# Gated linear attention with a folded feed-forward: K laid out by tokens with transposing DMAs, and running products over two chunks

## The chip, the cores and the metric

The kernel runs on one core of a Trainium2 chip. Its time is the device time of one execution in microseconds (us). The engines are named as in the profile: PE (TensorE) does matrix products, with PEld for its weight loads; DVE (VectorE), ACT (ScalarE) and POOL (GpSimd) work on elements; SP (SyncE) issues the DMA transfers. Each engine takes its instructions in the order in which the program gives them, and waits on semaphores for the results of the others. SBUF is the on-chip memory of 128 partitions, PSUM the eight banks that PE writes to.

## The reference

The first part is a gated linear recurrence for 4 batches, 8 heads, 768 steps and a head dimension of 48. Its result, with the heads side by side (3072 tokens of 384 numbers), goes through a feed-forward layer without a nonlinearity other than a product.

```python
f = 1.0 / (1.0 + np.exp(-f_logit))
state = np.zeros((B, H, D, D), dtype=np.float32)
for t in range(S):
    state = f[:, :, t, :, None] * state + np.einsum('bhd,bhe->bhde', k[:, :, t], v[:, :, t])
    y[:, :, t] = np.einsum('bhd,bhde->bhe', q[:, :, t], state)
...
a = x @ w1          # x: 3072 x 384, w1 and w2: 384 x 1024
b = x @ w2
h = a * b @ w3      # 1024 x 1024
return (h @ w_out).astype(np.float32)   # 1024 x 384
```

All of it is in 32-bit floats.

## The kernel before

**Recurrence.** The 768 steps of a batch are cut into 6 chunks of 128 tokens, 24 chunks (`NU`) in all, numbered u through the four batches. The 8 heads lie as 4 pairs: one head of a pair on partitions 0 to 47, the other on 64 to 111 (R = 112 rows), the four pairs side by side along the columns (4 x 128 = 512 columns, `NQ`). Within a chunk the decays are running products. A chunk's *front* makes them (`front`, L521 to L559): ACT takes the sigmoid of f (tile `gate`), a scan on DVE runs the product P forward over each head's 128 tokens (`fwd`), a small copy on ACT keeps its last column (`lasts`), a reciprocal sets the start of a second scan on DVE that runs R backward (`bwd`), and two products on DVE give Q = q * P and K = k * R, each into a tile of its own.

PE needs K twice: as it is for the products of K and Q (`pairs`, L584), and with tokens on the partitions for the update of the state (`update`, L690). For the second, PE itself transposes each head pair's 128 columns against an identity (`turn`, L598, four matrix products a chunk into a bank of PSUM), and ACT copies the bank to the tile `kt` (L731).

From chunk 4 on the PE work of neighbouring chunks is joined in *visits* (`visit` in `rest`): the visit of chunk u has half of the products of masked pairs with v (`values`, L658), the pairs of chunk u + 1, the other half of the values, the part from the state (`from_state`, L677), and the update of chunk u + 1. ACT copies the pairs out of PSUM (L707), POOL sets those after the diagonal to 0 (L713). On DVE the state is carried by `mid` and S (L763, L766) and multiplied by the gain G (L822), which POOL makes from `lasts` and the next chunk's first gate (L813). The result goes out by ACT (`ys`, L849), and two DMAs through DRAM turn it to the layout of the feed-forward (`yt`, then `xt`).

**Feed-forward.** The tokens are worked in 6 blocks of 512. w3 and w_out are first multiplied with each other on PE (L1471, eight groups of 16 matrix products, called the folding here) into `wc`, so that a block needs x with w1 and w2 (the up products), their elementwise product, and that with `wc` (the down products). Blocks use Strassen-like schemes, so sums and differences of weights and of x are made on DVE: those of the folded weights are the four of L1518 (`wc_sums`), which need all eight pieces of the folding.

**The order.** All tasks are given to a list scheduler, `Plan`, with an engine, an estimated cost, dependencies, a priority and the buffers they take. It picks the task that can start first by its estimates and so fixes the order of the instructions on each engine; on the chip the engines then wait for each other as it comes. The priorities of the recurrence follow `need(u)`, a due time of 60 + 14.5 (u - 4) from chunk 4 on. Where the plan has PE idle, the program puts dummy matrix products on the tile `floor` there (`idle`, L402), one for each 0.43 us of the gap.

Buffers: two gates, three q, two k and two f tiles, two K and three Q tiles, all of 112 x 512. Later in the program the same memory holds sums of weights (`homes`, `W_SUMS`).

Of the kernel before, what the change touches and what calls it, by code (L numbers as in the profile page):

```python
# [45 lines left out]
P = 128  # L46
C = 128
# [12 lines left out]
NQ = HP * C  # L60
NPE = 2
# [18 lines left out]
SURE_W = 2.0  # L80
NEED = (0.0, 1.0, 2.0, 3.0)
# [16 lines left out]
NFRONT = 12  # L98
# [28 lines left out]
FLOOR = 2.0**-60  # L127
RANGE = 2.0**-40
# [167 lines left out]
def ranged(ctx, tc, q, k, f_logit, v, w1, w2, w3, w_out, out, ident, w12, wc, left):  # L296
# [17 lines left out]
    floors = keep.tile([P, NQ], F32, name="floor")  # L314
    floor = floors[0:R]
    spare = keep.tile([P, NQ], F32, name="back")
    back = spare[0:R]
    gates_ = [keep.tile([P, NQ + 1], F32, name=f"gate{i}") for i in range(2)]
    inputs = [[keep.tile([P, NQ], F32, name=f"{nm}{i}") for i in range(n)] for nm, n in (("q", 3), ("k", 2), ("f", 2))]
    gate = [t[0:R] for t in gates_]  # L320
    qs, ks, fs = ([t[0:R] for t in ts] for ts in inputs)
    both = keep.tile([P, 2 * WIDE], F32, name="A")
    flat = [both[:, i * WIDE : i * WIDE + WIDE] for i in range(2)]
    masked = [t.rearrange("p (r h c) -> p r h c", r=2, h=HP) for t in flat]
    diag = [t[:, 0 : 2 * HP * W].rearrange("p (r h c) -> p r h c", r=2, h=HP) for t in flat]
    mids = [t[0:R, 2 * HP * W : 2 * HP * W + HP * D].rearrange("p (h d) -> p h d", d=D) for t in flat]
    firsts = [keep.tile([P, TB], F32, name=f"a{i}") for i in range(2)]
    sb = [t[0:R, 0 : HP * R].rearrange("p (h r) -> p h r", r=R) for t in firsts]
    lasts = keep.tile([R, NU, HP], F32, name="lasts")
# [23 lines left out]
    early = abp.tile([P, KH, TB], F32, name="ab")[0:R]  # L353
    ks += [early[:, 0], early[:, 1]]
    fs += [early[:, 2], early[:, 3]]
    qs.append(at(12288, NQ)[0:R])
    dns = {nm: at(12288 + DH * i, DH) for i, nm in enumerate(("m1", "u2", "u3"))}

    homes = [lambda t=t: t[:, 0:NQ] for t in [floors] + gates_ + inputs[0] + inputs[1] + inputs[2]]
    homes += [lambda p=p, nm=nm: p.tile([P, NQ], F32, name=nm) for p, nm, n in ((one, "fwd", 1), (one, "bwd", 1), (work, "K", 2), (work3, "Q", 3), (work3, "ys", 3)) for _ in range(n)]  # L360
# [16 lines left out]
    plan.pools["t"][0:4] = [aside] * 4  # L377
    moving = plan.add("PE", 0.0, lambda: None, takes=["ab"], prio=-1e9)
    coming = plan.add("PE", 0.0, lambda: None, takes=["ab"], prio=-1e9)
# [29 lines left out]
    def setup():  # L409
        E = mybir.EngineType  # L410
        tc.mark_branch_hint_location("general", hint="LikelyTaken", engines=[E.SP, E.DVE, E.PE, E.Activation, E.Pool])
        nc.scalar.activation(warm, nc.const_aps.tensor(0.0, (R, 1), F32), AF.Sigmoid)
        for i in range(2):
            if i == 0:
                nc.gpsimd.memset(ks[i][32:64], 0.0)
                nc.gpsimd.memset(qs[i][32:64], 0.0)
                make_identity(nc, ident)
            else:
                nc.gpsimd.memset(fs[i][32:64], 30.0)
        nc.gpsimd.memset(early[32:64, 2:4], 30.0)  # L420
        nc.gpsimd.memset(early[32:64, 0:2], 0.0)
        nc.gpsimd.memset(qs[2][32:64], 0.0)
        nc.gpsimd.memset(qs[3][32:64], 0.0)
        nc.vector.memset(floor, FLOOR)
        nc.vector.memset(heads(floor)[:, :, 0], 1.0)
        nc.vector.memset(back, 0.0)
        for t in gate:
            nc.vector.memset(t[:, NQ : NQ + 1], 0.0)
        nc.vector.memset(ks[1][32:64], 0.0)
        nc.vector.memset(qs[1][32:64], 0.0)  # L430
        for t in sb:
            nc.vector.memset(t, 0.0)

        nc.gpsimd.memset(perm, 0.0)
# [22 lines left out]
    def need(u):  # L457
        return NEED[u] if u < 4 else 60 + 14.5 * (u - 4)
# [21 lines left out]
    def front(u):  # L480
# [3 lines left out]
        ask = n0 - 30 if u in (0, 1) or u > 3 else turn_of(str(u))  # L484
        ask = [ask, ask + 0.5, ask + 1.0, n0 - (28.2, 28.2, 28.2, 28.2, 12)[min(u, 4)] if u in (0, 1) or u > 3 else ask + VLATE[u - 2] if u in (2, 3) else ask + 1.2]

        def load(dst, src):
            def emit():
                if dst is fs[0] and u == 0:
# [8 lines left out]
        fu, qu, ku = (x[u if u < 4 else u % n] for x, n in ((fs, 2), (qs, 3), (ks, 2)))  # L498

        def free(n, *names):  # L500

            if u < 4:
                return []
            return asked[8:9] + [tk[u - n if u - n >= 4 else u % n][nm] for nm in names]

        since = n0 - AHEAD if 4 < u < 8 else 0.0
        t["lf"] = moves(2, 197, 300, load(fu, f_logit), free(2, "g"), ask[0], since=since)
        t["lk"] = moves(2, 197, 300, load(ku, k), free(2, "k"), ask[1], since=since)
        t["lq"] = moves(2, 197, 300, load(qu, q), free(3, "q"), ask[2], since=since)

        def load_v():
# [4 lines left out]
            1, 197, 320, load_v, [] if u == 3 else past(u, 4 if u in (4, 5, 6) else 3, "v", "s"),  # L516
            ask[3],
        )

        def gates():  # L520
            nc.scalar.activation(gate[u % 2][:, 0:NQ], fu, AF.Sigmoid)  # L521

        t["g"] = plan.add("ACT", 0.65, gates, [t["lf"]] + past(u, 2, "r") + past(u, 3, "G"), n0)
        if u % NCH and "G" in tk[u - 1]:
            tk[u - 1]["G"]["deps"].append(t["g"])

        def forward():
            s["P"] = one.tile([P, NQ], F32, name="fwd")[0:R]
            nc.vector.tensor_tensor_scan(s["P"], gate[u % 2][:, 0:NQ], floor, 0.0, ALU.mult, ALU.max)  # L529

        t["p"] = plan.add("DVE", 1.25, forward, [t["g"]] + past(u, 1, "q", "i", "l"), n0)
# [6 lines left out]
        def ends():  # L538
            nc.vector.reciprocal(heads(back)[:, :, C - 1], heads(s["P"])[:, :, C - 1])
# [3 lines left out]
        def scale_q():  # L543
            s["Q"] = work3.tile([P, NQ], F32, name="Q")[0:R]
            nc.vector.tensor_tensor(s["Q"], qu, s["P"], ALU.mult)

        t["q"] = plan.add("DVE", 0.72, scale_q, [t["p"], t["lq"]] + past(u, 3, "v", "a"), n0 + QLATE, shared=True)

        def backward():
            s["R"] = one.tile([P, NQ], F32, name="bwd")[0:R]  # L550
            nc.vector.tensor_tensor_scan(  # L551
                s["R"][:, ::-1], gate[u % 2][:, NQ:0:-1], back[:, ::-1], 0.0, ALU.mult, ALU.max
            )

        t["r"] = plan.add("DVE", 1.25, backward, [t["i"]] + past(u, 1, "k"), n0)

        def scale_k():
            s["K"] = work.tile([P, NQ], F32, name="K")[0:R]
            nc.vector.tensor_tensor(s["K"], ku, s["R"], ALU.mult)  # L559

        t["k"] = plan.add("DVE", 0.72, scale_k, [t["r"], t["lk"]] + past(u, 2, "a", "t"), n0, shared=True)
        if u in (2, 3):
            t["k"]["frees"].append(coming)
# [160 lines left out]

    def turning(u):

        s, t = st[u], tk[u]

# [24 lines left out]
    def middle(u):  # L753
# [4 lines left out]
        def emit():  # L758
# [10 lines left out]
            "DVE", 0.36 if closes else 0.72, emit, [t["s"], t["m"]] + ([] if opens else past(u, 1, "d")) + past(u, 2, "v"), need(u) - 5,  # L769
        )  # L770

    def rest(u):
# [13 lines left out]
        else:  # L786
            middle(u)
            more = u + 1 < NU and u >= SOLO
            after = tk[u + 1] if more else {}

            def visit():
# [10 lines left out]
                "PE", 0.15 + 0.46 * (2 - 0.5 * opens + 2 * more), visit,  # L802
                [t["c"], t["lv"], t["mid"]] + past(u, 1, "y", *([] if opens else ["d"])) + [after[nm] for nm in ("q", "k", "e", "lv") if after],
                n0 - 998, slack=0.8,
            )
            if after:
                after["a"] = after["s"] = t["v"]
                paired(u + 1)

        if not closes:  # L810
            def gains():
                s["G"] = work.tile([R, HP], F32, name="G")
                nc.gpsimd.tensor_tensor(s["G"], lasts[:, u], heads(gate[(u + 1) % 2][:, 0:NQ])[:, :, 0], ALU.mult)  # L813
# [3 lines left out]
            )  # L817

# [24 lines left out]
        def outcome():  # L843
            s["ys"] = work3.tile([P, NQ], F32, name="ys")[0:R].rearrange("p (h c) -> p h c", c=C)
# [8 lines left out]
            "ACT", 0.8, outcome, [t["v"]] + past(u, 3, "z"),  # L853
# [43 lines left out]
    fronts = plan.add("none", 0.0, lambda: None)  # L897
# [9 lines left out]
    def ffn(n):  # L907
# [203 lines left out]
        def many_sums():  # L1111
            for k, (i, o, j, h) in enumerate(W_SUMS if not w_nodes else []):
                def emit(i=i, o=o, j=j, k=k):
                    nc.vector.tensor_tensor(w_view(4 * KM + k), w_view(i), w_view(j), op(o))
                w_nodes.append(plan.add("DVE", 0.69, emit, [over if h >= NFRONT else fronts] + w_nodes[-1:], W_SOON + 0.1 * k, since=W_SINCE + W_STEP * k))
# [123 lines left out]
        def down(i):  # L1239
# [88 lines left out]
            n0 = 100 * n + 90 + i + 60 * (n > 1) + 30 * (n == NB - 2)  # L1328
# [234 lines left out]
    def judge():  # L1563
        low = work.tile([R, 1], F32, name="low")
        nc.vector.tensor_reduce(out=low, in_=lasts, axis=AX.XY, op=ALU.min)
        zero = work.tile([R, NU], F32, name="zero")
        nc.vector.tensor_scalar(zero, ysum, 0.0, None, ALU.mult)
        nil = work.tile([R, 1], F32, name="nil")
        nc.vector.tensor_reduce(out=nil, in_=zero, axis=AX.X, op=ALU.add)
        nc.vector.tensor_scalar(nil, nil, 0.0, None, ALU.is_equal)  # L1570
        good = work.tile([P, 1], F32, name="good")
# [11 lines left out]
    def heard():  # L1583
        row = work.tile([1, P], F32, name="row")
# [3 lines left out]
    def decided():  # L1588
        least = work.tile([1, 1], F32, name="least")
# [4 lines left out]
    for u in range(NU):  # L1594
        if u <= SOLO:
            front(u)
        if NPE <= u <= SOLO:
            turning(u)
            begin(u)
        if u >= SOLO and u + 1 < NU:  # L1600
            front(u + 1)
# [6 lines left out]
        if u == NU - 1:  # L1608
# [4 lines left out]
            fronts["deps"] += [tk[u][nm] for nm in ("r", "k", "q")] + [tk[u - 1]["G"]]  # L1613
# [405 lines left out]
```

## Time and profile before

| | |
|---|---|
| runs, in us | 461.73, 459.99, 458.59 |
| median | 459.99 |
| the profiled execution | 458.04 |
| its span (first to last instruction) | 456.2 |
| clock of PE in it | 1.00 |

The busy times of an engine are sums over its instructions and can overlap with waits of others, so only a row of the chain that ended last, or a stretch in which one engine never stands still, tells what sets the end. The profile has three stretches that matter here: the folding from 60 to 120 us, the rest of the recurrence to 257 us, and products of the feed-forward alone from there to the end. Rows of groups give line, engine, operation, names and shapes, the count, busy time and mean of one; the rest of a row is idle time of that engine ahead of the group, with what ended it.

### The profile page before, as it was taken

What the parts mean: (1) busy time and instruction counts of PE and PEld (TensorE: products, weight loads), DVE (VectorE), ACT (ScalarE), POOL (GpSimd) and SP (SyncE); (2) the same over time, 40 slices, a digit from 0 to 9 for tenths busy, and PEclk for the clock granted to TensorE, in tenths of its full rate; (3) what the DMA queues carried; (4) which work ended last, traced back from release to release, by engine and by line L of the source; (5) the groups of instructions that cost most, each with busy time, mean ns of one, the idle gap of its engine ahead of it and who ended that gap; (6) DMA issues with size and microseconds to landing.
All of it is one profiled execution on the core that took longest, in us unless ns stands there. A gap on an engine that the chain in (4) does not pass through costs nothing.

```text
span 456.2 us, 11781 instructions
## 1 busy us (share of the span) xinstructions
PE 448.7 (98%) x4792; PEld 392.5 (86%) x4792; DVE 371.1 (81%) x651; ACT 212.0 (46%) x473; POOL 69.1 (15%) x90
## 2 busy tenths in 40 slices
PE   7999999999999999999999999999999999999996
PEld 6788886666899888889999888899899988889996
DVE  8997899999898999989999699885659466767641
ACT  4565344432234453443323256665665666675300
POOL 9341000131222531223223000000000000000000
PEclk9999999999999999999999999999999999999999
DMA  6897898833236666356323502446365612233111
GB/s 178 268 339 249 300 340 284 271 108 105 71 100 196 180 175 162 105 155 184 97 73 82 147 16 78 138 141 205 132 194 172 204 60 96 91 93 92 37 69 39
DMA packets 43308, 68.74 MB, mean 151 GB/s; under 512 B 5217, under 2 KB 28386, under 8 KB 42226
## 3 DMA queue, kind: packets, MB, share of 16 engines
q1 hardware_dynamic: 43250, 67.95, 48.6%
q8 instruction: 38, 0.62, 0.6%
q14 instruction: 20, 0.16, 0.1%
HBM read 58.88 MB, written 9.04 MB: 149 GB/s over the span
## 4 chain that ended last, share of the span: by engine, by line
PE 95%; DVE 1%; SPq 1%; DMA 1%; POOL 0%; issue 0%; POOLq 0%; DVEq 0%
PE f L902 25%; PE l L1153 15%; PE f L998 13%; PE f L1153 12%; PE f L1471 9%; PE l L902 9%; PE py L658 3%; PE pa L584 2%; PE f L598 2%; PE py L677 2%; PE pa L690 2%; PE f L402 1%; SPq L495 1%; DMA ab<-in_k_dram 1%; DVE K L559 0%
## 5 line engine op out<-in xcount | busy, mean ns | idle before, releaser
L713 POOL TENSOR_SCALAR_AFFINE_SELECT A<-A 64x512 f32<-64x512 f32 (+1 forms) x46 | 46.2, 1004 | 107.8 <-ACT A L707 105.7
L1471 PE MATMUL f<-place 128*128 128x384 f32 x128 | 42.4, 487 | 0.0
L902 PE MATMUL f<-xt,w 128*128 128x256 f32 x192 | 42.1, 380 | 0.0
L902 PEld LDWEIGHTS f<-xt,w 128*128 128x128 f32 x192 | 36.3, 190 | 5.0
L1471 PEld LDWEIGHTS f<-place 128*128 128x128 f32 x128 | 23.9, 190 | 15.5
L902 PE MATMUL f<-place 128*128 128x192 f32 x176 | 31.9, 327 | 0.0
L998 PE MATMUL f<-xt,w 128*128 128x256 f32 x120 | 31.3, 380 | 0.0
L551 DVE TENSOR_TENSOR_SCAN bwd<-gate,back 112x512 f32<-112x512 f32 x24 | 30.4, 1267 | 0.7
L529 DVE TENSOR_TENSOR_SCAN fwd<-gate,floor 112x512 f32<-112x512 f32 x24 | 30.0, 1251 | 1.2 <-ACT gate L521 0.3
L902 PEld LDWEIGHTS f<-place 128*128 128x128 f32 x176 | 28.9, 190 | 0.4 <-issue 0.2
L849 ACT ACTIVATE ys<-py 112x512 f32<-112x512 f32 x22 | 13.1, 597 | 32.4 <-PE py L677 29.9
L1407 ACT ACTIVATE place<-place 128x512 f32<-128x512 uint32 (+2 forms) x24 | 21.4, 890 | 9.7 <-DMA place<-in_w_dram 8.7
L998 PEld LDWEIGHTS f<-xt,w 128*128 128x128 f32 x120 | 22.5, 190 | 2.9
L902 PE MATMUL f<-wc,ab 128*128 128x192 f32 x128 | 23.6, 328 | 0.0
L813 POOL TENSOR_TENSOR G<-lasts,gate 112x4 f32<-112x4 f32 x20 | 12.3, 614 | 72.3 <-ACT lasts L534 28.7
L902 PEld LDWEIGHTS f<-wc,ab 128*128 128x128 f32 x128 | 21.2, 190 | 0.3
L521 ACT ACTIVATE gate<-f 112x512 f32<-112x512 f32 x22 | 13.9, 631 | 16.4 <-DVE bwd L551 7.2
L902 PE MATMUL l<-place 128*128 128x192 f32 x112 | 19.8, 326 | 0.0
L658 PEld LDWEIGHTS py<-A,vt 64*64 64x64 f32 (+1 forms) x672 | 13.3, 127 | 7.3 <-issue 6.3
L998 PE MATMUL f<-place 128*128 128x256 f32 x72 | 19.1, 386 | 0.0
L902 PEld LDWEIGHTS l<-place 128*128 128x128 f32 x112 | 18.5, 190 | 0.1
L658 PE MATMUL py<-A,vt 64*64 64x64 f32 (+1 forms) x672 | 18.0, 223 | 0.2
(288 smaller groups left out, 1063.4 us busy)
## 6 DMA issues: line engine op xcount, KB each, us to landing
place<-in_w_dram SPq DMA_DIRECT2D x21, 512.0 KB, 5.9
A<-in_w_dram SPq DMA_DIRECT2D x19, 512.0 KB, 4.0
place<-in_w_dram SPq DMA_DIRECT2D x8, 1024.0 KB, 6.3
q<-in_q_dram SPq DMA_DIRECT2D x46, 96.0 KB, 2.9
vt<-in_v_dram SPq DMA_DIRECT2D x23, 192.0 KB, 2.9
out_dram<-o SPq DMA_DIRECT2D x23, 192.0 KB, 2.8
k<-in_k_dram SPq DMA_DIRECT2D x44, 96.0 KB, 2.4
yt<-ys SPq DMA_DIRECT2D x44, 96.0 KB, 2.9
```

Source lines behind the costliest of these rows:

```text
L521: nc.scalar.activation(gate[u % 2][:, 0:NQ], fu, AF.Sigmoid)
L529: nc.vector.tensor_tensor_scan(s["P"], gate[u % 2][:, 0:NQ], floor, 0.0, ALU.mult, ALU.max)
L551: nc.vector.tensor_tensor_scan(s["R"][:, ::-1], gate[u % 2][:, NQ:0:-1], back[:, ::-1], 0.0, ALU.mult, ALU.max)
L658: done = nc.tensor.matmul(y_block(u, hp, par, half)[p0 : p0 + w], lhsT=s["v"][half * W : half * W + W, h * D : h * D + w], rhs=s["A"][half ...
L713: nc.gpsimd.affine_select(out=a, in_=a, pattern=pattern, compare_op=ALU.is_ge, fill=0.0, base=0, channel_multiplier=-1,)
L813: nc.gpsimd.tensor_tensor(s["G"], lasts[:, u], heads(gate[(u + 1) % 2][:, 0:NQ])[:, :, 0], ALU.mult)
L849: nc.scalar.activation(ys, py, AF.Copy, accum_out=ysum[:, u : u + 1])
L902: nc.tensor.matmul(out_, lhsT=lhs[i], rhs=rhs[i], start=start and i == 0, stop=i == len(lhs) - 1, skip_group_check=True,)
L998: nc.tensor.matmul(q[nm][:, which * TH : which * TH + TH], lhsT=lhs[i](which), rhs=rhs[i], start=start and which == 0 and i == 0, stop=i = ...
L1153: nc.tensor.matmul(banks[g, c][:, which * TH : which * TH + TH], lhsT=lhs, rhs=x_node(a), start=first and which == 0, stop=True, skip_grou ...
L1407: nc.scalar.activation(part_.bitcast(F32), part_, AF.Copy, bias=2.0, scale=2.0**-51)
L1471: nc.tensor.matmul(w3s["p", jc], lhsT=w3s[jc][:, kc * P : kc * P + P], rhs=wos[:, kc], start=(kc == 0), stop=(kc == KF - 1),)
```

## The change

From chunk 4 on the fronts are made for two chunks at once (`front_of_two`). Its gate, k and q tiles hold both chunks (112 x 1024); the running products go over 256 tokens, so that both chunks of the two share one reference point: an even chunk there has no G and no product of S with G any more. Backward products are written over the gates, Q and K over q and k. There are three q tiles, two k tiles and two gate tiles of this size.

From chunk 5 on, K gets its tokens onto partitions without PE (`crossing`): ACT splits the 32-bit words into their upper and lower halves (16 bits each) in the staging tile `apart`, a transposing DMA from SP's queue turns the eight 112 x 128 pieces into `halves`, and ACT merges the halves into `kt`. Both tiles exist once. Chunks 0 to 4 are transposed on PE as before.

From chunk 7 on (`TURN`) the visit of chunk u has the pairs of chunk u + 2 in place of u + 1; the pairs of chunk 8 come as a task of their own ahead of the visit of chunk 7. `mid` of u now also waits for the copy of the pairs of u + 1. The due times start 12 us earlier (48 in place of 60), a down product's priority changes for one block, and the sums of weights wait for parts of the old fronts' buffers apart from each other.

```diff
+ALONE = 4
+TURN = 7
...
     def need(u):
-        return NEED[u] if u < 4 else 60 + 14.5 * (u - 4)
+        return NEED[u] if u < 4 else 48 + 14.5 * (u - 4)
...
+    def front_of_two(e):
...
+        P_, R_ = running[0:R, 0:N2], gate[0:R, 1 : N2 + 1]
+        def gates():
+            nc.scalar.activation(gate[0:R, 0:N2], gate[0:R, 0:N2], AF.Sigmoid)
+        def forward():
+            nc.vector.tensor_tensor_scan(P_, gate[0:R, 0:N2], back, 0.0, ALU.mult, ALU.max)
+        def scale_q():
+            to = by_head(qu)
+            nc.vector.tensor_tensor(to, to, by_run(P_), ALU.mult)
+        def backward():
+            nc.vector.tensor_tensor_scan(R_[:, ::-1], R_[:, ::-1], back[:, ::-1], 0.0, ALU.mult, ALU.max)
+            nc.vector.memset(heads2(back)[:, :, 2 * C - 1], 0.0)
+        def scale_k():
+            to = by_head(ku)
+            nc.vector.tensor_tensor(to, to, by_run(R_), ALU.mult)
...
+    def crossing(u):
+        def split():
+            nc.scalar.copy(apart.rearrange("p (two n) -> p two n", two=2), s["K"].bitcast(U16).rearrange("p (n two) -> p two n", two=2))
+        def crossed():
+            nc.sync.dma_start_transpose(halves.rearrange("p (g r) -> p g r", r=R), apart)
+        def merged():
+            s["kt"] = work.tile([P, HP, R], F32, name="kt")
+            to = s["kt"].rearrange("p h r -> p (h r)").bitcast(U16).rearrange("p (n two) -> p two n", two=2)
+            nc.scalar.copy(to, halves.rearrange("p (two n) -> p two n", two=2))
+        n0 = need(u)
+        t["t"] = plan.add("ACT", 1.27, split, [t["k"]] + past(u, 1, "c2"), n0 - 50)
+        t["c2"] = moves(1, 229, 200, crossed, [t["t"]] + past(u, 1, "e"), n0 - 100, SURE_K)
+        t["e"] = plan.add("ACT", 1.13, merged, [t["c2"]] + past(u, 2, "s"), n0 - 50)
...
     def turning(u):
+        if u > SOLO:
+            crossing(u)
+            return
...
+            to = u + 2 if u >= TURN else u + 1
+            two = tk[to] if to < NU and more else {}
+            if u == TURN:
+                ahead = tk[u + 1]
+                ahead["a"] = plan.add("PE", 0.46, lambda: pairs(u + 1), [ahead["q"], ahead["k"], t["m"], t["mid"]], n0 - 999, slack=0.8)
...
                 values(u, 1)
-                if more:
-                    pairs(u + 1)
+                if two:
+                    pairs(to)
                 values(u, 0)
                 from_state(u)
                 if more:
                     update(u + 1)
...
-        if not closes:
+        if not closes and u >= ALONE and u % 2 == 0:
+            t["d"] = t["mid"]
+        elif not closes:
...
-            n0 = 100 * n + 90 + i + 60 * (n > 1) + 30 * (n == NB - 2)
+            n0 = 100 * n + 90 + i + 60 * (n > 0) + 30 * (n == NB - 2)
```

In the rows of the order, a line of the program stands first, then the instruction, its output and inputs by name and a shape. On PE, at the end of the folding, before (`py` is a visit's bank, `pa` that of pairs and updates, `place` and `wc` hold weights):

```order
L677 MATMUL py<-Q,A 48x64 x8
L690 MATMUL pa<-vt,kt 48x48 x16
L902 MATMUL f_1248<-xt,w_59 128x256 x3
L902 MATMUL f_1259<-xt,w_59 128x256 x3
L902 MATMUL f_1271<-xt,w_59 128x256 x3
L902 MATMUL f_1277<-xt,w_59 128x256 x3
L402 MATMUL f_1289<-floor 128x256 x2
L902 MATMUL f_1292<-wc,ab 128x192 x4
```

And in the changed kernel (L779 is `from_state`, L792 the update, L1611 the folding, L686 `pairs`, L416 the dummies, L760 the values):

```order
L779 MATMUL py<-q_98,A 48x64 x8
L792 MATMUL pa<-vt,kt 48x48 x16
L1611 MATMUL f_1196<-place 128x384 x8
L416 MATMUL f_1234<-floor 128x256 x4
L686 MATMUL pa<-q_99,k_101 64x64 x16
L416 MATMUL f_1265<-floor 128x256 x4
L760 MATMUL py<-A,vt 64x64 x2
```

The pairs of chunk 8 and the visit of chunk 7 have moved ahead of the first product with `wc`, and eight dummies stand around them where two stood (a ninth is further up).

On DVE, ahead of the differences of `wc` (L1504 are sums of w1 and w2, L529 and L551 the two scans, L1518 the differences), before:

```order
L1504 TENSOR_TENSOR place<-w_59,place 128x512
L1504 TENSOR_TENSOR place<-w_59 128x512
L529 SCALAR_TENSOR_TENSOR fwd<-gate_95,floor 112x512
L539 RECIPROCAL back<-fwd 112x4
L551 SCALAR_TENSOR_TENSOR bwd<-gate_95,back 112x512
L1518 TENSOR_TENSOR place<-wc 128x768
L1518 TENSOR_TENSOR place<-wc,place 128x768
```

And in the changed kernel (L1644 are the sums of w1 and w2, L632 the forward scan of two chunks, L888 and L891 `mid` and S, L962 S with G, L1658 the differences):

```order
L1644 TENSOR_TENSOR place<-w_59,place 128x512
L1644 TENSOR_TENSOR place<-w_59 128x512
L632 SCALAR_TENSOR_TENSOR run<-gate_96,back 112x1024
L888 TENSOR_TENSOR A<-pa,S 112x192
L891 TENSOR_TENSOR S<-pa,A 112x192
L962 TENSOR_TENSOR S<-S,G 112x192
L1658 TENSOR_TENSOR place<-wc 128x768
L1658 TENSOR_TENSOR place<-wc,place 128x768
```

A scan for two chunks, and the carry of chunk 7, now stand ahead of the differences; the fronts of earlier chunks stand further up in both.

On ACT, in the recurrence after the folding, before (L731 copies a transposed K, L1039 copies up products out of their banks, L707 the pairs, L849 a result):

```order
L521 ACTIVATE gate_96<-f_103 112x512
L731 COPY kt<-f_1706 128x448
L1039 COPY a_105<-f_1712 128x512
L534 COPY lasts<-fwd 112x4
L521 ACTIVATE gate_95<-f_102 112x512
L849 ACTIVATE ys,ysum<-py 112x2x2x128
L707 COPY A<-pa 128x512
L1039 COPY a_106<-f_1712 128x512
```

And in the changed kernel (L840 is the merge, L832 the split, L1179 copies up products, L989 a result, L809 the pairs):

```order
L1179 COPY a_105<-f_1542 128x512
L840 COPY kt<-halves 128x2x448
L1179 COPY a_106<-f_1542 128x512
L832 COPY A<-k_101 112x1024
L989 ACTIVATE ys,ysum<-py 112x2x2x128
L809 COPY A<-pa 128x512
L1179 COPY place<-f_1542 128x512
```

The merge and the split stand between copies that empty PE's banks, with one such copy between the merge of a chunk and the split of the next.

More of the change, by code (lines that the diff above doesn't have):

```diff
@@ L60 @@
 NQ = HP * C
+N2 = 2 * NQ
+ALONE = 4
+TURN = 7
 NPE = 2
@@ L496, in load @@
             return emit
[L498 to L509, printed above, removed]
+        t["lf"] = moves(2, 197, 300, load(fu, f_logit), [], ask[0])
+        t["lk"] = moves(2, 197, 300, load(ku, k), [], ask[1])
+        t["lq"] = moves(2, 197, 300, load(qu, q), [], ask[2])
         def load_v():
```

235 lines of the change are left out of this document (157 added, 78 removed).

## The prediction

> **What bounds the kernel now.** I read the page first: span, busy times, clock, and the share of each line in the chain that ended last.
>
> ```profile
> span 456.2 us, 11781 instructions
> PE 448.7 (98%) x4792; PEld 392.5 (86%) x4792; DVE 371.1 (81%) x651; ACT 212.0 (46%) x473; POOL 69.1 (15%) x90
> PEclk9999999999999999999999999999999999999999
> PE 95%; DVE 1%; SPq 1%; DMA 1%; POOL 0%; issue 0%; POOLq 0%; DVEq 0%
> ```
>
> PE is busy for 448.7 of 456.2 us at full clock and makes 95% of the chain. So PE work taken away shortens the span by as much, and any time in which PE stands still is added. Next, the view of waits for PE (wait, total, times, longest), of which these are two of the three rows:
>
> ```profile
> PE f L402 <- DVE floor L425: 1.7, 1, 1.7
> PE py L598 <- DVE K L559: 0.5, 1, 0.5
> ```
>
> Both belong to the start. Nothing else holds PE: every other engine is early, and the question is which one stays early. The windows view gives it by stage (length, then busy time and count of PE, PEld, DVE, ACT, POOL, then clock, DMA share, GB/s); 60 to 120 us is the folding of w3 with w_out, 120 to 257 the rest of the recurrence beside up and down products, 257 to 452 products alone.
>
> ```profile
> 60.00:120.00 60.00, 60.00 (x608) 40.42 (x607) 56.97 (x75) 23.29 (x43) 9.54 (x10) 1.00 0.63 199
> 120.00:257.00 137.00, 136.90 (x2599) 123.70 (x2598) 125.62 (x225) 52.09 (x127) 37.86 (x46) 1.00 0.50 135
> 257.00:452.00 195.00, 194.99 (x1015) 180.08 (x1013) 135.51 (x283) 106.56 (x244) 0.00 (x0) 1.00 0.35 112
> ```
>
> In the folding DVE is busy for 56.97 of 60 us: it is second to PE and has 3 us to spare. ACT is idle for more than half of each of these stages.
>
> **Term 1: the transposes leave PE.** The chain in order of time (start, length, what), around the visit of chunk 5 and the end of the folding, and for 120 to 257 us the heading of the same view, shares by line:
>
> ```profile
> 78.44 0.39 PE f L598 x4
> 103.49 0.38 PE py L658 x11
> 103.87 0.47 PE pa L584 x30
> 105.02 0.36 PE pa L690 x32
> 105.38 0.53 PE f L598 x4
> 123.29 0.86 PE f L402 x4
> 124.15 3.94 PE f L902 x23
> ```
>
> ```profile
> by line: PE f L998 41.0%; PE f L902 29.7%; PE py L658 7.7%; PE pa L584 5.4%; PE py L677 5.2%; PE f L598 5.1%; PE pa L690 4.2%; PE f L1153 1.3%; PE f L402 0.6%; issue 0.0%
> ```
>
> Transposes take 5.1% of these 137 us, 7.0 us for 16 chunks, 0.44 us each; single pieces are 0.39 behind products and 0.53 behind an update. Chunks 5 to 23 lose theirs: 19 x 0.44 = 8.3 us. The bounds: 19 x 0.39 = 7.4, and by the busy time of all such rows, quoted next, 88 of 12.6 us, 4 to a chunk, 0.57 a chunk, so 10.9.
>
> ```profile
> L598 PE MATMUL f<-ident,K 112*128 112x112 f32 x88 | 12.6, 266 | 0.5 <-DVE K L559 0.5
> L551 DVE TENSOR_TENSOR_SCAN bwd<-gate,back 112x512 f32<-112x512 f32 x24 | 30.4, 1267 | 0.7
> L529 DVE TENSOR_TENSOR_SCAN fwd<-gate,floor 112x512 f32<-112x512 f32 x24 | 30.0, 1251 | 1.2 <-ACT gate L521 0.3
> L559 DVE TENSOR_TENSOR K<-k,bwd 112x512 f32<-112x512 f32 x22 | 16.9, 770 | 0.4
> L545 DVE TENSOR_TENSOR Q<-q,fwd 112x512 f32<-112x512 f32 x23 | 16.2, 704 | 0.0
> L944 DVE TENSOR_TENSOR ab<-f,ab 128x256 f32<-128x256 f32 x16 | 6.7, 422 | 2.9 <-PE f L902 2.9
> L763 DVE TENSOR_TENSOR A<-pa,S 112x192 f32<-112x192 f32 x19 | 6.5, 345 | 0.1
> L766 DVE TENSOR_TENSOR S<-pa,A 112x192 f32<-112x192 f32 x18 | 6.4, 358 | 0.6
> L822 DVE TENSOR_TENSOR S<-S,G 112x192 f32<-112x192 f32 x18 | 7.3, 404 | 0.6
> ```
>
> **Term 2: the end of the folding is given back.** The first down products need the four differences of wc on DVE (L1518), which ended just in time before. The timeline of DVE there, and at one of the ordinary pairs of products:
>
> ```profile
> 119.44 1.40 DVE L1518 TENSOR_TENSOR place<-wc,place 128x768 f32<-128x768 f32 x1
> 71.64 0.69 DVE L559 TENSOR_TENSOR K<-k,bwd 112x512 f32<-112x512 f32 x1
> 72.25 0.68 DVE L545 TENSOR_TENSOR Q<-q,fwd 112x512 f32<-112x512 f32 x1
> ```
>
> The last difference ends at 120.84, PE reaches the product at 124.15 after two dummy matmuls of 0.43 each (L402). Read off the order, DVE has more to do ahead of the differences than before, since a front now serves two chunks and pairs run a chunk further ahead: three more chunks of forward scans (3.75), one more of backward (1.27), two K (1.54), two Q (1.41), two products L944 (0.84), and mid and S of chunk 7 (0.70) less one product with G (0.40): +9.1 us. Against that, 13 instructions over 512 elements become parts of instructions over 1024 and save the fixed part of one. Two rows bound that: a start 0.61 behind the other where one lasts 0.69 leaves no more than 0.08, and 0.69 at 512 against 0.345 at 192 elements gives 0.14 by a straight line; I take 0.10, 1.3 us. DVE is then 7.8 us later, at 128.6. PE, in its own order, does without the two dummies (0.86) and three chunks of transposes (1.32), and has the visit of chunk 7 (105.38 - 103.49 = 1.89) and pairs of chunk 8 (0.47) ahead of the product: 124.33. Between the two lie 4.3 us. Since 0.86 of such filling was there before, the step costs 4.3 - 0.86 = 3.5 us. The order shows the same from its side: nine dummies (one, four, four) instead of two, 7 x 0.43 = 3.0 us of PE time that is spent whether DVE is late or not, so 3.0 is the lower end. The upper is 5.2, with all instructions saved at nothing (1.3) and the transposes at 0.53 (0.3 more). A rule bears on how such a gap is filled: the Trainium skill (TensorE: Matmul & The Clock Gate, Part 1) has PE's clock fall to half after an idle window of about 3.4 us. This trace cannot show it, since its slices keep full clock and PE never stands so long; with the nine dummies in the gap the sum is the same by the rule as without.
>
> **What I cost at nothing, and its cover.** The crossing adds to 19 chunks, on ACT, a split and a merge of as many elements as the second row here, and takes the copy in the first away; then a DMA between two SBUF tiles, 229 KB, bounded by the rows under them (kilobytes each, median us to landing).
>
> ```profile
> L731 ACT COPY kt<-f 128x448 f32<-128x448 f32 x22 | 11.8, 537 | 7.0 <-PE f L598 6.8
> L1407 ACT ACTIVATE place<-place 128x1024 f32<-128x1024 uint32 x8 | 9.3, 1165 | 7.3 <-DMA place<-in_w_dram 7.3
> vt<-in_v_dram SPq DMA_DIRECT2D x23, 192.0 KB, 2.9
> xt<-yt SPq DMA_DIRECT2D x22, 192.0 KB, 3.4
> place<-in_w_dram SPq DMA_DIRECT2D x8, 1024.0 KB, 6.3
> ```
>
> ACT: 2 x 1.17 - 0.54 = 1.8 us a chunk, 16 chunks, 29 us in the 137 us of the second window: 52 become 81. The idle 56 us cover it, unless merge stands ahead of an evacuation for which PE waits (a rival below). The transfer: no row shows one that transposes. Its ends are 2.9 and 6.3; I take 3.4, the row of nearest size and shape. K is ready a chunk or more ahead, so 3.4 + 1.2 + 1.2 + a copy of 0.6 lies in the 8.2 us that a chunk lasts (below). SP issues 19 of these and 40 fewer k and q loads (four fewer for each of ten pairs). Behind a crossing that waits for its split stand loads, yt stores and xt gathers; none was waited for by PE before, and a split that is late by one ACT task (0.6) delays them by no more. On DVE, K and Q in place, merged scans and no G products for even chunks save about 1 us a pair after 120 us, where DVE is not the bound. Bigger f, k and q loads, POOL's ten fewer G, later pairs and the start (other memsets, one dummy fewer) I put at 0, with 0.4 either way for the start. The wait of mid for m of the next chunk holds one DVE instruction behind an ACT copy of 0.58 that a whole chunk precedes: 0, cover 8 us.
>
> **Sum.** -8.3 + 3.5 = -4.8. The profiled execution took 458.04 us, so 453.2; the median of the three runs shown is 459.99, 1.95 more, so 455.2, 1.0% less. Of its own bounds: -10.9 + 3.0 gives 452.1, -7.4 + 5.2 gives 457.8.
>
> **Rivals.**
> 1. *All of it arrives.* Transposes at their busy time (0.57) and no more given back than the seven dummies: 452.1, and a little less (451) if DVE's savings free a bank earlier. For it: PE is the bound everywhere. Against: the chain's pieces are 0.39 to 0.53.
> 2. *The folding gives back all.* DVE has 3 us to spare in 60 us and gets 7.8 more; if PE stops for the K or Q of chunks 6 to 8 as well as for the differences, or the crossing of chunk 5 is late behind 1 MB w3 loads (6.3 us to landing, DMA share 0.63), the lateness counts almost in full: -8.3 + 7.8 = -0.5 at 459.5, up to 462. For it: the stage's DVE load. Against: nothing ahead of PE there was late by more than 0.5 before.
> 3. *The crossing paces the chunks, slower.* There is one staging tile and one tile of halves, and ACT takes instructions in order: landing, merge, one or no other copy, split, next issue. That cycle is L + 1.17 + 0.6 + 1.17 = L + 2.9, with L the landing time. The visits of chunks 5 and 23 start at 103.49 and at the first row here, so a chunk lasts (251.57 - 103.49)/18 = 8.2 us, and the cycle is longer from L = 5.3 on.
>
> ```profile
> 251.57 0.44 PE py L658 x11
> ```
>
> From there each us costs 18: at 5.6 the gain is gone (455.2 + 5.4 = 460.6), at 6.0, near the 6.3 of the largest transfer, 455.2 + 12.6 = 467.8. For it: the size of the transfer is known, its kind is in no row; a wait in merge also holds evacuations. Against: 3.4 has 1.9 to spare, and even that row taken half as slow again (an estimate, 5.1) stays below 5.3. The Trainium skill speaks for this rival in one place (Advanced Engine Details and Errata, DGE: Hardware vs Software), which rates the transposes of the queues that SyncE issues as the less efficient kind, with no figure. In another (the same page, X-Bar Transpose (TRN2)) it has transposing transfers as fast as regular ones; by the second the sum stays at 455.2, by the first it would move towards 467.8. No run here shows either yet.
>
> **How the numbers follow.** The forecast's case (452 to 458) has 0.47, rival 1 0.15, rival 2 0.18, rival 3 0.20 (0.03 of it within 1%). About 1%, 455.4 to 464.6, is what a measurement of this kernel can tell from no change: 0.28 of the forecast's case lies below 455.4, with rival 1 0.43 for faster; 0.19 + 0.18 + 0.03 = 0.40 for the same; 0.17 for slower. The range 451 to 465 leaves out rival 3's upper part.
>
> **What would show it.** Right, term 1: no L598 row after chunk 4 and about 0.4 us less between visits. Term 2: nine dummies or a wait of PE just ahead of the first product with wc, with the last difference on DVE at 127 to 130. Crossing hidden: landing below 5 us and no wait of PE on kt. Wrong: PE rows that wait for ACT kt or for a bank whose copy stands behind a merge, visits more than 8.2 apart, or a clock below full.

## The result, and the profile after

| | us |
|---|---|
| changed kernel, median of four runs | 503.97 (500.45 to 507.17) |
| kernel before, median of four runs | 459.94 (458.59 to 461.73) |
| ratio, with its 95% interval | 1.095 (1.086 to 1.105) |
| profiled execution of the changed kernel | 500.45, span 498.7 |

The change makes the kernel 9.5% slower. The forecast was 455.2, with 0.17 for slower and 465 as the upper end of the range. Two of the four runs of e1 below (480.39 and 484.00 us) were in a slower state, at a granted clock of 0.98 against 0.99, so its time is the median of the other two. The page of the changed kernel: span, busy times, the clock and the load of the DMA engines in 40 slices, and the chain by engine.

```profile
span 498.7 us, 11583 instructions
PE 459.2 (92%) x4728; PEld 397.3 (80%) x4728; DVE 362.1 (73%) x610; ACT 235.6 (47%) x472; POOL 62.6 (13%) x81
PEclk9999999799998899899999999999999999999999
DMA  6876959857244448864687444274336532332111
PE 71%; DMA 13%; issue 6%; ACT 3%; POOL 3%; SPq 2%; DVE 1%; ACTq 0%; POOLq 0%; DVEq 0%
```

PE has gone from 98% to 92% busy: it stands for 498.7 - 459.2 = 39.5 us, where it stood for 7.5. PE's busy time has not fallen either, though 76 transposes left it and only 12 instructions of dummies came: it is 10.5 us longer, and in some slices the granted clock is below full, which no slice was before. DMA, which had 1% of the chain, has 13%. All of it happens beside the recurrence: from 300 to 452 us PE is busy for 151.9 of 152 us, as before. What PE waited for, the four longest of 17 rows:

```profile
PE f L1138 <- ACT place L1179: 5.3, 1, 5.3
PE pa L686 <- DVE A L888: 4.5, 1, 4.5
PE f L1042 <- DVE place L1422: 4.0, 1, 4.0
PE f L1042 <- ACT place L1416: 3.0, 1, 3.0
```

No row dominates: PE waits a few us each time for copies that empty its banks and for carries on DVE. These wait in turn. The views of waits for ACT and for SP (the DMA queue's own):

```profile
ACT gate L625 <- DMA gate<-in_f_logit_dram: 45.2, 8, 11.1
ACT kt L840 <- DMA halves<-A: 28.9, 10, 5.6
```

```profile
SPq L600 <- DMA gate<-in_f_logit_dram: 22.4, 14, 4.5
```

The sigmoid waited for f for 45.2 us, in eight places (7.1 us before, in five), and the merge for the crossing for 28.9. The last row is the one to see: SP, about to issue an f load (L600), waits for another f load to land. The load of f for two chunks is four DMAs, two per chunk, and the second chunk's go to columns that lie between those of the first, in the same tile. They are issued only when the first chunk's have landed, and SP's queue stands meanwhile. This is called the false wait below, since the two chunks' columns do not overlap. One such place, from the timelines of SP, of ACT and of PE (start, length, what, and in brackets the idle time ahead of it):

```profile
224.58 5.66 SPq L600 DMA_DIRECT2D gate<-in_f_logit_dram  x4
230.33 1.27 SPq L835 DMA_TRANSPOSE halves<-A  x1
```

```profile
232.62 1.06 ACT L625 ACTIVATE gate<-gate 112x1024 f32<-112x1024 f32 x1 [6.82 <-DMA gate<-in_f_logit_dram]
...
233.93 1.19 ACT L840 COPY kt<-halves 128x896 uint16<-128x896 uint16 x1
234.99 0.57 ACT L1179 COPY place<-f 128x512 f32<-128x512 f32 x1
```

```profile
235.61 1.22 PE L1138 MATMUL f<-place 128*128 128x256 f32 x2 [5.34 <-ACT place L1179]
```

Four issues take 5.66 us, ACT stands for 6.82 us ahead of the sigmoid of a pair that PE does not need yet, and behind it in ACT's order, after the merge of a crossing that SP could issue only at 230.33, is the copy L1179 that PE needs now: 5.34 us lost on PE. The crossing itself landed as forecast (kilobytes are not given for it; median us to landing):

```profile
k<-in_k_dram SPq DMA_DIRECT2D x20, 192.0 KB, 3.8
q<-in_q_dram SPq DMA_DIRECT2D x20, 192.0 KB, 4.9
halves<-A SPq DMA_TRANSPOSE x19, 3.5
```

It took 3.5 us; the k and q loads, twice as large as before, took 3.8 and 4.9 in place of 2.4 and 2.9.

The clock follows the stops. The windows of the changed kernel around one of them, with the clock as the third number from the end:

```profile
78.00:84.00 6.00, 5.82 (x40) 4.79 (x38) 5.88 (x7) 1.86 (x5) 0.00 (x0) 1.00 1.08 283
84.00:90.00 6.00, 2.26 (x8) 1.35 (x8) 3.88 (x5) 3.36 (x6) 2.42 (x2) 0.88 0.99 374
90.00:94.00 4.00, 3.76 (x6) 2.18 (x7) 3.96 (x7) 1.14 (x1) 1.18 (x2) 0.50 1.09 333
```

PE works for 2.26 of 6 us, and in the 4 us that follow its clock is 0.50. The mean over the span is 0.975, so up to 0.025 x 498.7 = 12.5 us of the loss is the clock and not the waiting itself.

### The profile page after: what moved, and what is told of

It reads as the page before. It is cut to its first block, busy times and chain, and to the rows that moved or that the text cites. A ratio compares the mean times of both kernels' runs of the same rounds, so it can differ in the third digit from the quotient of the medians.

```text
span 498.7 us, 11583 instructions
## 1 busy us (share of the span) xinstructions
PE 459.2 (92%) x4728; PEld 397.3 (80%) x4728; DVE 362.1 (73%) x610; ACT 235.6 (47%) x472; POOL 62.6 (13%) x81
## 4 chain that ended last, share of the span: by engine, by line
PE 71%; DMA 13%; issue 6%; ACT 3%; POOL 3%; SPq 2%; DVE 1%; ACTq 0%; POOLq 0%; DVEq 0%
PE l L1293 12%; PE f L1042 12%; PE f L1293 12%; PE f L1138 10%; PE l L1042 8%; PE f L1611 8%; DMA gate<-in_f_logit_dram 5%; DMA place<-in_w_dram 4%; PE py L760 2%; DMA q<-in_q_dram 2%; PE pa L686 2%; PE py L779 1%; DMA halves<-A 1%; PE pa L792 1%; POOL ab L453 1%
## 5 line engine op out<-in xcount | busy, mean ns | idle before, releaser
L1611 PE MATMUL f<-place 128*128 128x384 f32 x128 | 44.6, 511 | 2.1 <-ACT ab L1079 2.1
L1611 PEld LDWEIGHTS f<-place 128*128 128x128 f32 x128 | 25.3, 200 | 20.0 <-ACT ab L1079 2.4
L1042 PE MATMUL f<-place 128*128 128x192 f32 x192 | 35.8, 338 | 4.9 <-DVE place L1422 4.0
L1042 PEld LDWEIGHTS f<-place 128*128 128x128 f32 x192 | 33.2, 198 | 5.3 <-DVE place L1422 4.2
L840 ACT COPY kt<-halves 128x896 uint16<-128x896 uint16 x19 | 22.8, 1202 | 29.1 <-DMA halves<-A 28.9
L625 ACT ACTIVATE gate<-gate 112x1024 f32<-112x1024 f32 x10 | 10.6, 1059 | 45.2 <-DMA gate<-in_f_logit_dram 45.2
L653 DVE TENSOR_TENSOR_SCAN gate<-gate,back 112x1024 f32<-112x1024 f32 x10 | 23.3, 2330 | 0.4
L632 DVE TENSOR_TENSOR_SCAN run<-gate,back 112x1024 f32<-112x1024 f32 x10 | 22.8, 2283 | 0.9 <-ACT gate L625 0.8
L832 ACT COPY A<-k 112x1024 uint16<-112x1024 uint16 x19 | 19.8, 1042 | 7.1 <-DVE k L660 7.1
L1042 PE MATMUL f<-wc,ab 128*128 128x192 f32 x96 | 19.7, 353 | 3.0 <-ACT place L1416 3.0
L416 PE MATMUL f<-floor 112*128 112x256 f32 x60 | 17.5, 442 | 5.3 <-ACT ys L989 2.3
L989 ACT ACTIVATE ys<-py 112x512 f32<-112x512 f32 x22 | 13.1, 594 | 17.4 <-PE py L779 15.4
L760 PEld LDWEIGHTS py<-A,vt 64*64 64x64 f32 (+1 forms) x672 | 14.0, 127 | 8.9 <-issue 6.7
L686 PE MATMUL pa<-q,k 48*64 48x64 f32 x704 | 15.7, 225 | 5.9 <-DVE A L888 4.5
```

Source lines behind the costliest of these rows:

```text
L632: nc.vector.tensor_tensor_scan(P_, gate[0:R, 0:N2], back, 0.0, ALU.mult, ALU.max)
L653: nc.vector.tensor_tensor_scan(R_[:, ::-1], R_[:, ::-1], back[:, ::-1], 0.0, ALU.mult, ALU.max)
L686: nc.tensor.matmul(s["pa"][half * W : half * W + W, par, hp * W : hp * W + W], lhsT=s["K"][rows(par), cols], rhs=s["Q"][rows(par), cols], ...
L760: done = nc.tensor.matmul(y_block(u, hp, par, half)[p0 : p0 + w], lhsT=s["v"][half * W : half * W + W, h * D : h * D + w], rhs=s["A"][half ...
L832: nc.scalar.copy(apart.rearrange("p (two n) -> p two n", two=2), s["K"].bitcast(U16).rearrange("p (n two) -> p two n", two=2))
L840: nc.scalar.copy(to, halves.rearrange("p (two n) -> p two n", two=2))
```

## The experiments

All times are medians of four runs, of two for e1; the kernel before, run on the same chip, had 459.49 beside the first four, 459.35 beside the next four, 459.61 beside e9 to e11 and 458.82 beside e12 to e14. Line numbers of these kernels are up to two lower than those of the changed kernel where f is loaded by two DMAs (L598 is L600 there). Apart from e1 and e12, which keep the order of the kernel that they are compared with, each edit also makes the planner choose another order.

**e1: f of a pair in two DMAs.** Nothing else is changed; the order of all engines is the same.

```diff
-            for k in range(2):
-                to, from_ = (
-                    x.rearrange("p (h c) -> p h c", h=HP) for x in (gate[:, 0:N2], f_logit[e + k].rearrange("two d n -> (two d) n"))
-                )
-                for a, b, n in ((0, 0, 64), (64, D, D)):
-                    nc.sync.dma_start(to[a : a + n, :, k * C : k * C + C], from_[b : b + n])
+            to = gate[:, 0:N2].rearrange("p (h k c) -> p h k c", h=HP, k=2)
+            from_ = f_logit[e : e + 2].rearrange("k two d (h c) -> (two d) h k c", h=HP)
+            for a, b, n in ((0, 0, 64), (64, D, D)):
+                nc.sync.dma_start(to[a : a + n], from_[b : b + n])
```

> The f load of a pair of chunks is made of two DMAs (one for each range of partitions, both chunks in it) in place of four; every other instruction and the order of all engines stay. Theory A (the second chunk's f DMAs wait in SP's queue until the first chunk's have landed, 22.4 us of SP's waits, and hold crossings, k, q and weight loads behind them): that wait is gone, SP issues f for a pair in about 1.2 us instead of 4.2 to 7.1, ACT's wait for gate falls from 45 us to under 15, and the time to 455 to 470. Theory B (the crossing, with its merge in front of ACT's evacuations, is what holds PE): 495 or more, ACT still waits some 29 us for halves. Theory C (pairs two chunks ahead lengthen the chain of buffers): 495 or more.

Measured: 474.1 (473.18 and 475.05), 29.9 us less than the changed kernel. SP has no wait of an f load for an f load any more; the issue for a pair is one row of 1.33 us on SP's timeline, here with its neighbour:

```profile
132.52 1.33 SPq L598 DMA_DIRECT2D gate<-in_f_logit_dram  x2
133.94 0.57 SPq L491 DMA_DIRECT2D vt<-in_v_dram  x1
```

```profile
PE 450.1 (95%) x4728; PEld 391.2 (83%) x4728; DVE 361.5 (76%) x610; ACT 236.5 (50%) x472; POOL 62.1 (13%) x81
```

PE stands for 473.3 - 450.1 = 23.2 us and its busy time is 9.1 us shorter with the same instructions, as the mean clock is 0.992. So theory A names the largest part, 30 of the 44 us, but it fell short of its own numbers: 474.1 is above the 470 that it allowed, ACT still waits 31.8 us for f, and 14.6 us against the kernel before are left. The edit also halves the f loads that SP issues for a pair, from four to two; no run separates that from the wait.

**e2 and e4: K transposed on PE in all chunks**, with the four f loads (e2) and with two (e4).

```diff
     def turning(u):
-        if u > SOLO:
+        if u > NU:
             crossing(u)
             return
```

> The changed kernel with K transposed on PE in all chunks, no crossing; fronts of two chunks and pairs two ahead stay. Theory A: SP still waits for its f DMAs, so the time stays near the changed kernel's, 490 to 510 (up to 8.3 us of transposes come back on PE, up to 25 us of SP's issues leave). Theory B: 455 to 470.

> Both the f load of two DMAs and K transposed on PE in all chunks. Theory A: 458 to 470, the transposes' 8.3 us more than without the second edit, or less if the crossing costs something of its own. Theory B: 455 to 470 as well, but no better than the run with PE transposes alone. Theory C: 495 or more.

Measured: e2 504.12, ratio 1.097 (1.094 to 1.101); e4 487.35, ratio 1.059 (1.055 to 1.062). Theory B falls: without any crossing the changed kernel is as slow as with them. Against e1, e4 is 13.2 us slower, so the crossing gains at least what it was meant to once the false wait is gone; with the false wait in place it gains nothing (504.12 against 503.97). That PE then waits for loads anyway is the likely reason, not a tested one. But e4 is also above the range of theory A: 27.9 us over the kernel before, with no crossing and no false wait.

**e3: the pairs of chunk u + 1 in every visit** (`TURN = 24` in place of 7).

> The changed kernel with the pairs of chunk u + 1 in every visit. Theories A and B: 495 to 510, no change beyond 2%. Theory C: 460 to 475.

Measured: 508.42, ratio 1.105 (1.102 to 1.109). By this run pairs two chunks ahead are not what costs the time. But this variant computes other values than the reference, and which step of it does that was not found, so its time is taken only as a sign against theory C.

**e5, e6, e7, e8: what holds SP's queue in e1.** e5 has another order, made with longer loads; e6 a fourth vt tile; e7 the old due times; e8 the fourth tile and an order made with longer loads and 1.35 us for issuing a crossing. The edits against e1:

```diff
 e5
-        t["lf"] = moves(4, 460, 300, load_f, asked[8:9] + before, ask[0], since=since)
+        t["lf"] = moves(4, 460, 300, load_f, asked[8:9] + before, ask[0], 1.0, since=since)
...
 e6
-    loads = ctx.enter_context(tc.tile_pool(name="loads", bufs=3))
+    loads = ctx.enter_context(tc.tile_pool(name="loads", bufs=4))
...
 e7
-        return NEED[u] if u < 4 else 48 + 14.5 * (u - 4)
+        return NEED[u] if u < 4 else 60 + 14.5 * (u - 4)
...
 e8, with the edit of e6 and the margins of e5
-        t["c2"] = moves(1, 229, 200, crossed, [t["t"]] + past(u, 1, "e"), n0 - 100, SURE_K)
+        t["c2"] = moves(3, 229, 200, crossed, [t["t"]] + past(u, 1, "e"), n0 - 100, 0.4)
```

> The f load of two DMAs, and the plan told that loads for two chunks land later than it assumed (f by 1 us, k and q by 2 us, after the measured 4.1 to 5.9 us); the operations are the same, their order on the engines follows the plan. Theory D (what is left of the loss comes from an order made with too short transfers, which the engines then cannot keep): ACT's wait for gate falls from 32 us to under 20, 460 to 470. Theory E (SP's queue: vt loads wait there for visits on PE, 43 us, and hold the crossings behind them): no change beyond 1%, 473 to 482.

> The f load of two DMAs, and four vt tiles instead of three, so that a vt load waits for the visit of a chunk further back. Theory E: SP's wait for py falls from 43 us (60 to 270 us) to under 20, crossings are issued within 2 us of their split, and the time is 460 to 470. Theory D: 473 to 482.

> The f load of two DMAs, and the due times of the recurrence as before the change (60 in place of 48): only priorities, so only the order. Theory F (the recurrence was pulled ahead into the stage in which weights are loaded, at a DMA share of 0.82 from 60 to 120 us): 460 to 470. Theories D and E: 473 to 485.

> The f load of two DMAs, four vt tiles, and the plan told of the landing times and of 1.35 us for issuing a crossing (0.45 before). Theories D and E together: 455 to 465. If neither holds: above 473.

Measured: e5 490.15 (ratio 1.068, 1.060 to 1.077), e6 474.10 (1.030, 1.024 to 1.035), e7 490.00 (1.063, 1.056 to 1.070), e8 470.07 (1.019, 1.012 to 1.026). Theory F falls: with the old due times the kernel is 16 us slower than e1, not faster. The fourth vt tile does what theory E asked of SP's queue but not of the time. SP's waits of vt loads for the products of a visit with v, first in e1, then in e6:

```profile
SPq L491 <- PE py L758: 31.7, 6, 9.9
SPq L491 <- PE py L758: 8.6, 4, 5.8
```

The merge's wait for the crossing falls with them, from 24.3 to 6.5 us, and yet e6 (474.10) is as slow as e1 (474.1). So those waits of vt loads are not shown to cost anything. e8 is the best version of the study, between the ranges given for it, and still 10.7 us above the kernel before. In e5 ACT's wait for f falls to 17.3 us, as theory D wanted, while the time rises above every range given: a plan with truer loads does not by itself make a better order.

**e9, e10, e11: the operations and buffers of e1 in three other orders**, made with longer loads, yt and xt, earlier asks for f, k and q, and later vt loads (e11: pairs two ahead from chunk 8 on). The core of e9:

```diff
-        tk[u]["lv"] = moves(1, 197, 320, load_v, past(u, 4 if u in (4, 5, 6) else 3, "v", "s"), need(u) - 12)
+        tk[u]["lv"] = moves(1, 197, 320, load_v, past(u, 4 if u in (4, 5, 6) else 3, "v", "s"), need(u) - 0)
...
-        ask = [n0 - 30, n0 - 29.5, n0 - 29.0]
+        ask = [n0 - 36, n0 - 36 + 0.5, n0 - 36 + 1.0]
```

> The f load of two DMAs; same operations and buffers, another order: the plan is told longer landings (f 0.5, k 1, q 2, crossing 0.5, yt 0.5 and xt 1 us more), asks for f, k and q 6 us sooner and gives vt loads a due time 12 us later, so that fewer loads that wait for a visit stand ahead of a crossing in SP's queue. Theory D (the rest of the loss is an order that real landings break): 460 to 468, ACT's wait for halves under 12 us, PE's idle time before 300 us under 12 us. Theory G (the fronts of two chunks and the crossing cost PE time in any order): 474 or more, as with the order of the first repair.

> As before with other margins (f 1, k 2, q 2, yt 1, xt 1 us more; crossing's issue 0.9 us; vt due 18 us later). Theory D: 460 to 468. Theory G: 474 or more.

> As before with other margins (f 1.5, k 2, q 1, crossing 0.5, xt 1.5 us more, vt due 12 us later), due times 13.5 us apart, and pairs two chunks ahead from chunk 8 on instead of 7. Theory D: 458 to 468. Theory G: 474 or more.

Measured: 482.45 (1.049, 1.043 to 1.054), 481.95 (1.051, 1.045 to 1.058), 485.89 (1.055, 1.050 to 1.061). All three miss theory D's range. In e9 the sigmoid's wait for f is still 30.2 us, and one stop of PE, 6.53 us long, shows the clock most plainly (windows of e9):

```profile
154.00:161.00 7.00, 0.47 (x2) 0.35 (x2) 4.65 (x9) 3.77 (x7) 1.31 (x2) 0.87 0.76 155
161.00:165.00 4.00, 4.00 (x14) 4.00 (x14) 3.42 (x6) 0.96 (x3) 0.32 (x1) 0.50 0.55 134
```

**e12, e13, e14: the parts once more, around e8.** e12 is e8 with the four f loads again (the lines taken out in e1), in the same order; e13 is e8 with PE transposes in all chunks (the edit of e2); e14 has crossings in even chunks alone.

```diff
-        if u > SOLO:
+        if u > SOLO and u % 2 == 0:
             crossing(u)
             return
```

> The kernel of the run with four vt tiles and told costs (470.1 us), with f of a pair loaded by four DMAs again, the order of all engines unchanged. Theory A (false wait in SP's queue): 485 to 505, SP waits for its own f DMAs again by 15 us or more. If the price of 26 us belonged to one order only: 468 to 475.

> The same kernel (470.1 us, f by two DMAs) with K transposed on PE in all chunks. Theory H (the crossings' load on the DMA engines is what is left of the loss): 455 to 467. Theory I (fronts of two chunks cost it; crossings still pay for themselves): 474 to 488.

> The same kernel with crossings in even chunks alone and K of odd chunks transposed on PE. Theory H: 458 to 468. Theory I: 472 to 480, between the run with all crossings and the one with none.

Measured: e12 477.40 (1.039, 1.032 to 1.046), e13 478.56 (1.043, 1.037 to 1.049), e14 473.68 (1.030, 1.023 to 1.036). The false wait costs 7.3 us in this order, between the two cases expected, though SP waits longer for it than in the changed kernel:

```profile
SPq L600 <- DMA gate<-in_f_logit_dram: 32.5, 11, 9.4
```

So the length of the wait does not set its price. That what is queued behind it does, and that with another order and a spare vt tile fewer things that PE needs soon stand there, is argued and was not tried by itself. Theory H falls: with no crossings the kernel is 8.5 us slower, with half of them 3.6, and both times lie in theory I's ranges. Crossings pay for themselves, about in proportion.

## Why the prediction was wrong, step by step

- **Term 1, the transposes leave PE (-8.3):** the mechanism was right, and so was the size, as far as the runs tell it. The runs that differ in it, and in what the order makes of it, give 13.2 (e1 and e4) and 8.5 (e8 and e13). In the kernel as changed it is worth nothing (e2).
- **Term 2, the end of the folding (+3.5):** the dummies are there, eight of the nine in two groups (four dummies are eight instructions), and DVE makes the differences from 142.06 on, beside the second group. The timelines of PE and DVE in the changed kernel:

```profile
138.11 1.89 PE L416 MATMUL f<-floor 112*128 112x256 f32 x8
142.00 1.99 PE L416 MATMUL f<-floor 112*128 112x256 f32 x8
```

```profile
144.85 1.40 DVE L1658 TENSOR_TENSOR place<-wc,place 128x768 f32<-128x768 f32 x1
```

  The last difference ends at 146.25, not between 127 and 130, since the whole stage was already late. The 3.5 us were not measured apart. (Its upper end adds up to 5.1, not 5.2: 3.5 + 1.3 + 0.3.)
- **"Bigger f, k and q loads ... I put at 0":** this is the step that failed, a term put at nothing without a look at what the loads wait for. I counted the DMAs of a pair (four, as before) but not what each had to wait for. The DMAs of the two chunks, whose columns interleave in one tile, were taken as independent; the second chunk's wait for the first's, in a queue that holds crossings, k, q and v loads behind them. Cost: 29.9 us in this order (e1), 7.3 in another (e12).
- **"K is ready a chunk or more ahead" and the crossing:** the landing time was right (3.4 forecast, 3.5 measured in the median), and rival 3, crossings that take more than 5.3 us as a rule, did not happen. But the cover was counted from the split, and the crossing is issued when SP comes to it. In e1 a split begins at 142.7 and its crossing at 153.7. Slow loads do to ACT what I feared of slow crossings: the sigmoid, like the merge, stands ahead of copies for which PE waits.
- **"The Trainium skill" on the crossing:** the page Advanced Engine Details and Errata, X-Bar Transpose (TRN2), has transposing transfers as fast as regular ones, DGE: Hardware vs Software those of SyncE's queue as less efficient. To the latency the first applies here (3.5 us against 3.9 for xt, 192 KB). To the load on the DMA engines it does not, as the last section shows; that was not what cost the time (e13).
- **The rule on the clock** (the Trainium skill, TensorE: Matmul & The Clock Gate, Part 1): I held that with dummies in the gap the rule changes nothing. But they cover only the gaps that the plan expects. In e9 PE stood for 6.53 us, longer than the 3.4 us of the rule, and the clock was 0.50 over the next 4 us, as the rule has it. In the changed kernel it was 0.50 from 90 to 94 us after two stops of only 1.64 and 2.07 us with 0.70 us of dummies between them, so there dummies and short stops were not enough to keep it up.
- **The rest is not settled.** Without the false wait and with PE transposes, what is left of the change, above all the fronts of two chunks, still costs 27.9 us (e4), 19.7 with a fourth vt tile and another order (e13). Shown not to be the cause: the crossing, pairs two ahead as far as e3 can be taken, due times that are too early. Not shown to be part of it: the vt loads in SP's queue, which waited far less in e6 than in e1 at the same time of the kernel. The clock is part of it by the profile: mean 0.984 in e4, 0.992 in e13, at most 7.8 and 3.8 us of their spans. Part of it lies where I allowed 0.4 us, at the start. The first 60 us of the kernel before, then of e8:

```profile
0.00:60.00 60.00, 56.82 (x576) 48.31 (x577) 52.66 (x70) 30.08 (x61) 21.68 (x35) 1.00 0.83 269
0.00:60.00 60.00, 51.47 (x543) 43.04 (x544) 46.12 (x68) 26.85 (x55) 19.90 (x35) 0.97 0.90 252
```

  PE stands there for 8.5 us in e8 and for 3.2 before, of 18.7 and 7.5 in all, and the first crossing is issued only at 68.8. One wait in it is for a gather of a result (`xt`), a transfer that PE did not wait for before:

```profile
PE f L1040 <- DMA xt<-yt: 3.3, 1, 3.3
```

  That gather is issued at 43.92, right behind the first f and k loads of two chunks; what delays it was not tried. A likely rest is that a tile of two chunks is loaded later and in one lump, and comes free later, since K, Q and the backward products are written over it; that was argued from the code and not tried. Orders matter: e1 and e5, with the same operations and buffers, lie 16 us apart. But none of the orders made here reaches the kernel before, which does not show that none could.

No version of the study is faster than the kernel before.

## What to carry to other kernels

When a load is cut into several DMAs, look at whether they write ranges of one tile that interleave: the second may wait for the first (ranges that do not interleave were not tried here), and in an in-order queue everything behind it waits too. How much that costs depends on the order: 29.9 and 7.3 us here. Price an edit not by the instructions that it adds but by the queue at which each has to wait, and give work that leaves a bound engine no credit until the loads that feed that engine are shown to keep ahead. A kernel whose bound engine is 98% busy has no room for lateness: a stop of a few us costs the stop and can cost, as at 90 to 94 us here, half of the clock for some us more.

## What the runs showed of the hardware that was not expected

A transposing DMA is short but heavy. e1 and e4 differ in 19 crossings; the DMA packets and the share of the 16 DMA engines, first of e1, then of e4:

```profile
DMA packets 67067, 73.84 MB, mean 156 GB/s; under 512 B 21889, under 2 KB 54018, under 8 KB 65986
q1 hardware_dynamic: 67010, 73.06, 58.1%
```

```profile
DMA packets 49436, 69.49 MB, mean 143 GB/s; under 512 B 4257, under 2 KB 36386, under 8 KB 48354
q1 hardware_dynamic: 49378, 68.70, 47.9%
```

A crossing is (67067 - 49436)/19 = 928 packets, all under 512 bytes, for 229 KB. By the shares it takes (0.581 x 473.3 - 0.479 x 487.2)/19 = 2.2 us of all 16 engines, 105 GB/s; by e8 and e13 it is 2.4 us. These differences hold other packets too, which take more or less time from run to run. The packets of 256 bytes, which only crossings have (896 each), add up to 1.6 us a crossing in the changed kernel and 2.2 in e8, so 105 to 146 GB/s. All transfers of e13, which has no crossing, come to 68.70 MB in 0.505 x 473.2 = 239 us, 287 GB/s. The Trainium skill (DMA: Bandwidth & Descriptors, Latency and other measured facts) has 261 GB/s for a transposing DMA with a strided middle dimension; this case shows 105 to 146. To issue one takes SP 1.26 us (median of 19 in the changed kernel), where a k or q load takes 0.43.
